# First block of a convolution and SiLU feed-forward kernel: the matrices' units from the third on issued from SP, the second block's input queued behind them

## The chip, the cores and the metric

One NeuronCore of one Trainium2 chip. The metric is device time in microseconds (us) of one execution; quoted times are medians of several runs. A profile is one execution taken by the hardware profiler; its span is 1.7 to 1.9 us shorter than the time of that run.

## The reference, cut to what matters

```python
# lightweight convolution along the sequence, 7 taps, one set of taps per head (8 heads of 24 channels)
out = np.einsum('hk,bskhg->bshg', softmax(weight), windows_of(x_padded))   # x: (8, 4096, 192)
# feed-forward on the 32768 rows of it
h = x @ w_in                          # w_in: (192, 2048), float64 as given
g = h * (1.0 / (1.0 + np.exp(-h)))    # SiLU
return (g @ w_out).astype(np.float32) # w_out: (2048, 192), float64 as given
```

The two weight matrices arrive as float64. The kernel loads their words and rounds them to float32 itself, in units: four for `w_in` and four for `w_out`.

## The kernel before

The 32768 rows are worked in 32 blocks of 1024. The first block is special. While TensorE multiplies it, the units of the matrices are still being loaded, rounded on VectorE and, for `w_in`, swapped between partition halves by a DMA (`ws<-wr`) that only the second block reads. From the second block on, everything is steady.

```python
tpool = tc.tile_pool(name="tp", bufs=3)   # raw words and rounding scratch share three buffers
psum  = tc.tile_pool(name="ps", bufs=8, space=PSUM)
...
def load(b):                 # input of block b: 12 loads of 64 KB in pieces of 128 bytes ("nat")
    ...
def load_in(j, queue):       # unit j of w_in: four loads of 192 KB ("raw")
    ...
def load_out(q, queue):      # unit q of w_out: two loads of 384 KB ("raw")
    ...
def round_in(j):
    rounded(wr[j]..., ("i", j), j < 2)              # VectorE (ScalarE helps for units 0 and 1)
    for e in range(2):
        nc.scalar.dma_start(                        # the swap, issued from ScalarE's queue
            out=ws[j][R * e : R * e + R], in_=wr[j][R - R * e : 2 * R - R * e])
...
def up_plain(b, j):          # matmuls of unit j into all 8 PSUM banks, then SiLU frees them
    ...
            if k == NK - 1:
                for e in range(2):
                    nc.scalar.activation(g[:, n, e, :], hs[a, n, e], AF.Silu)
...
load_in(0, nc.scalar)
load_in(1, nc.sync)
...
for k in range(NK):
    turn_in(0, k)            # transpose, convolve and spread ("dup") the first block's input
    ...
    spread(0, k)             # four SP copies of 128 KB
    if k == 0:
        round_in(0)
        load_in(2, nc.gpsimd)
round_in(1)
load_in(3, nc.gpsimd)
load(1)
for j in range(NJ):          # NJ = 4
    up_plain(0, j)
    if j + 2 < NJ:
        round_in(j + 2)
        load_out(j, nc.gpsimd)
    else:
        round_out(j + 2 - NJ)
        load_out(j, nc.gpsimd)
for j in range(2, NJ):
    round_out(j)
```

The text counts units from one: the "fourth unit" is `load_in(3)`, `round_in(3)`. In the profile, the lines are L123 (nat), L163 and L170 (raw), L109 (rounding), L217 (swap), L335 (dup), L373 (matmuls of `up_plain`), L383 (its SiLU), L503 (the first block's down projection), L409 and L464 (the steady blocks). A scheduler decides the order in each engine's queue.

Of the kernel before, what the change touches and what calls it, by code (L numbers as in the profile page):

```python
# [17 lines left out]
def kernel(  # L18
# [24 lines left out]
    nc = tc.nc  # L43
# [74 lines left out]
    def load(b):  # L118
        nat = nats[b] = xpool.tile([P, NK, TB // SQ, SQ], F32, tag="nat", name="nat")
        for k in range(NK):  # L120
            for i in range(P // SQ):
                c = R * k + SQ * (i % 2)
                (nc.sync if b or k or i % 2 else nc.scalar).dma_start(  # L123
                    out=nat[SQ * i : SQ * i + SQ, k, :, :],
                    in_=x_v[2 * b + i // 2][:, :, c : c + SQ],
                )
# [27 lines left out]
    def raw_tile(key):  # L154
        raws[key] = tpool.tile([P, 4 * TB], I32, tag="t", name="raw")[:, 0 : 2 * WC]
        return raws[key]

    def load_in(j, queue):
        raw = raw_tile(("i", j)).rearrange("p (a k c) -> p a k c", a=2, k=NK)
        for e in range(2):  # L160
            for a in range(2):
                c = 2 * P * (NM * a + 2 * j + e)
                queue.dma_start(  # L163
                    out=raw[R * e : R * e + R, a, :, :], in_=in32[:, :, c : c + 2 * P]
                )

    def load_out(q, queue):
        raw = raw_tile(("o", q)).rearrange("p (a e d) -> p a e d", a=2, e=2)
        for a in range(2):
            queue.dma_start(out=raw[:, a, :, :], in_=out32[a, q])  # L170
# [42 lines left out]
    def round_in(j):  # L213
        rounded(wr[j].rearrange("p a k c -> p (a k c)"), ("i", j), j < 2)

        for e in range(2):
            nc.scalar.dma_start(  # L217
                out=ws[j][R * e : R * e + R], in_=wr[j][R - R * e : 2 * R - R * e]
            )

    def round_out(q):
        rounded(wo[q].rearrange("p a e d -> p (a e d)"), ("o", q), False)
# [71 lines left out]
    def turn_in(b, k):  # L294
        if k == 0 and b:
            xt = xts[b] = xpool.tile([P, NK, pad + TB], F32, tag="xt", name="xt")
            if b * TT % S == 0:
                nc.gpsimd.memset(xt[0:R, :, 0:pad], 0.0)
            else:
                nc.gpsimd.tensor_copy(xt[0:R, :, 0:pad], tails.pop(b))  # L300
        xt = xts[b]
        pin(
            nc.vector.transpose(  # L303
                xt[:, k, pad : pad + TB], nats[b][:, k, :, :].rearrange("p k c -> p (k c)")
            )
        )
        if k == NK - 1:
            if b:
                nc.sync.dma_start(out=xt[R:P, :, 0:pad], in_=xt[0:R, :, TB : TB + pad])
            if (b + 1) * TT % S:  # L310
                tails[b + 1] = xpool.tile([R, NK, pad], F32, tag="tail", name="tail", bufs=2)
                nc.sync.dma_start(out=tails[b + 1], in_=xt[R:P, :, TB : TB + pad])

    def conv(b, k, i):

        src = xts[b][:, k, i : i + TB]
        dst = nats[b][:, k, :, :].rearrange("p k c -> p (k c)")
        tap = taps[:, k, i : i + 1]
        if i == 0:
            pin(nc.vector.tensor_scalar(dst, src, scalar1=tap, scalar2=None, op0=ALU.mult))  # L320
        else:
            pin(
                nc.vector.scalar_tensor_tensor(  # L323
                    out=dst, in0=src, scalar=tap, in1=dst, op0=ALU.mult, op1=ALU.add
                )
            )

    def spread(b, k):

        if k == 0:  # L330
            dups[b] = xpool.tile([P, 2, NK, TB], F32, tag="dup", name="dup")
        src = nats[b][:, k, :, :].rearrange("p k c -> p (k c)")
        for n in range(2):
            for e in range(2):
                nc.sync.dma_start(  # L335
                    out=dups[b][R * e : R * e + R, n, k, :], in_=src[R * n : R * n + R, :]
                )
# [25 lines left out]
    def up_plain(b, j):  # L363

        d = dups[b]
        outs = [(a, n) for a in range(2) for n in range(2)]
        hs = {(a, n, e): bank() for a, n in outs for e in range(2)}
        order = [(k, o) for k in range(NK) for o in outs]
        if j:
            order = [(k, o) for o in outs for k in range(NK)]  # L370
        for k, (a, n) in order:
            for e in range(2):
                nc.tensor.matmul(  # L373
                    hs[a, n, e],
                    rows(wr[j], e)[:, a, k, :],
                    rows(d, e)[:, n, k, :],
                    start=k == 0,
                    stop=k == NK - 1,
                )
            if k == NK - 1:  # L380
                for e in range(2):
                    g = g_tile(b, j, a)
                    nc.scalar.activation(g[:, n, e, :], hs[a, n, e], AF.Silu)  # L383
# [229 lines left out]
    for k in range(NK):  # L613
        turn_in(0, k)
        for i in range(K):
            conv(0, k, i)
        spread(0, k)
        if k == 0:
            round_in(0)
            load_in(2, nc.gpsimd)  # L620
    round_in(1)
    load_in(3, nc.gpsimd)
    load(1)
    for j in range(NJ):
        up_plain(0, j)
        if j + 2 < NJ:
            round_in(j + 2)
            load_out(j, nc.gpsimd)
        else:
            round_out(j + 2 - NJ)  # L630
            load_out(j, nc.gpsimd)
    for j in range(2, NJ):
        round_out(j)
    for s in plan[:NU]:
# [55 lines left out]
```

## Time and profile before

| | before |
|---|---|
| median of 3 runs | 2485.74 us (2484.02 to 2486.81) |
| span of the profiled run | 2482.4 us |
| TensorE busy | 2444.7 us (98%) |
| TensorE idle, all within the first 60 us | 21.5 + 1.84 + 0.31 + 2.51 + 1.35 us |
| half-clock stretches (before the last microseconds) | two, 29.96 to 33.37 and 43.62 to 47.03 us |

The lines on which the prediction rests stand in it. Four more lines of the timeline are needed later. Lines of the timeline give start and duration in us, then engine, line, operation and tile; in brackets stands the idle time before and what ended it. "ACTq" is an issue from ScalarE's queue.

```profile
39.84 1.12 ACTq L217 DMA_DIRECT2D ws<-wr  x2
40.99 1.28 ACT L383 ACT_TABLE_LOAD   x1 [5.01 <-DVE two L109]
42.28 4.03 ACT L383 ACTIVATE g<-ps 128x512 f32<-128x512 f32 x8
42.93 15.32 PE L373 MATMUL ps<-dup,wr 64*128 64x512 f32 x60 [2.51 <-ACT g L383]
```

The swap of the second unit sits in ScalarE's queue and waits for VectorE until 39.84. Only behind it come the table load and the first SiLU, and TensorE starts again at 42.93. The same pattern returns at 57.79 with the swap of the fourth unit; that is the wait the change is about.

### The profile page before, as it was taken

The numbers are of one execution on the slowest core, as the hardware profiler recorded it, in microseconds if no ns is written. First come the engines' busy times: TensorE is split into PE (matmuls) and PEld (weight loads), VectorE is DVE, ScalarE is ACT, GpSimd is POOL, SyncE is SP. The second block draws the span as 40 slices with busy tenths as digits, with TensorE's granted clock in tenths as the row PEclk, the third lists the DMA queues.
The fourth block names the chain that finished last, engine by engine and source line by source line (L and its number), as shares of the span: only waits on it lengthen the run. The fifth ranks groups of instructions, "written<-read, shape, count | busy, mean of one in ns | idle before, by whom it ended". The sixth has DMA issues, their size and how long they took to land.

```text
span 2482.4 us, 29776 instructions
## 1 busy us (share of the span) xinstructions
PE 2444.7 (98%) x11296; PEld 955.3 (38%) x11296; DVE 2043.7 (82%) x2748; ACT 968.8 (39%) x1747; POOL 69.9 (3%) x107
## 2 busy tenths in 40 slices
PE   5999999999999999999999999999999999999998
PEld 2334433344333344333433333443334433333332
DVE  8798888888888988888888889888888888898875
ACT  2144433344333444333443334443334433344432
POOL 3300000000000000000000000000000000000000
PEclk9999999999999999999999999999999999999999
DMA  7321122211222211222112222112221122221110
GB/s 149 73 47 31 35 52 51 41 37 35 43 52 43 46 32 35 51 52 40 38 35 43 52 43 47 31 35 52 51 40 38 34 43 52 43 45 33 35 39 13
DMA packets 450270, 110.78 MB, mean 45 GB/s; under 512 B 422304, under 2 KB 423968, under 8 KB 450128
## 3 DMA queue, kind: packets, MB, share of 16 engines
q1 hardware_dynamic: 444272, 101.26, 21.4%
q0 software_dynamic: 1600, 4.92, 0.8%
q10 hardware_dynamic: 4256, 2.72, 0.5%
q8 instruction: 88, 1.44, 0.3%
q14 instruction: 54, 0.44, 0.1%
HBM read 31.49 MB, written 25.17 MB: 23 GB/s over the span
## 4 chain that ended last, share of the span: by engine, by line
PE 97%; DVE 1%; DMA 1%; issue 0%; POOL 0%; ACTq 0%; ACT 0%; POOLq 0%; DVEq 0%
PE ps L409 47%; PE ps L464 47%; PE ps L503 2%; PE ps L373 1%; DVE two L109 0%; DVE nat L323 0%; DMA raw<-in_moe_w_in_dram 0%; DMA nat<-in_x_dram 0%; DVE mh L109 0%; DVE xt L303 0%; POOL raw L163 0%; DVE nat L320 0%; DVE u L550 0%; DVE cmb L550 0%; ACTq L217 0%
## 5 line engine op out<-in xcount | busy, mean ns | idle before, releaser
L464 PE MATMUL ps<-g,wo 128*64 128x512 f32 x2976 | 873.2, 593 | 0.0
L409 PE MATMUL ps<-dup,ws 64*128 64x512 f32 x2480 | 869.9, 589 | 0.0
L433 DVE TENSOR_TENSOR g<-u,ps 128x512 f32<-128x512 f32 x744 | 488.5, 680 | 117.0 <-PE ps L409 103.0
L409 PE MATMUL ps<-win,wr 64*128 64x512 f32 x1488 | 567.7, 589 | 0.0
L464 PEld LDWEIGHTS ps<-g,wo 128*64 128x64 f32 x2976 | 275.6, 137 | 572.2 <-issue 548.7
L430 ACT ACTIVATE g<-g 128x512 f32<-128x512 f32 x744 | 445.6, 631 | 88.1 <-DVE g L433 88.1
L409 PEld LDWEIGHTS ps<-dup,ws 64*128 64x128 f32 x2480 | 363.0, 187 | 292.0 <-issue 284.7
L464 PE MATMUL ps<-t,wx 128*64 128x512 f32 x992 | 466.1, 592 | 0.0
L323 DVE SCALAR_TENSOR_TENSOR nat<-xt,taps,nat 128x512 f32<-128x512 f32 x576 | 431.4, 749 | 11.9
L547 ACT COPY cmb<-ps 64x512 f32<-64x512 f32 (+1 forms) x93 | 54.1, 582 | 965.1 <-PE ps L464 964.3
L409 PE MATMUL ps<-dup,wr 64*128 64x512 f32 x992 | 419.9, 596 | 0.0
L424 ACT COPY u<-ps 128x512 f32<-128x512 f32 x496 | 278.2, 589 | 233.3 <-PE ps L409 233.0
L464 PE MATMUL ps<-t,wo 128*64 128x512 f32 x992 | 360.5, 592 | 0.0
L450 DVE TENSOR_TENSOR t<-g,t 128x1024 f32<-128x1024 f32 x248 | 303.6, 1224 | 60.6 <-PE ps L464 50.2
L409 PEld LDWEIGHTS ps<-win,wr 64*128 64x128 f32 x1488 | 233.4, 187 | 175.3 <-issue 146.9
L450 DVE TENSOR_TENSOR t<-g 128x1024 f32<-128x1024 f32 x248 | 299.3, 1218 | 0.0
L409 PE MATMUL ps<-win,ws 64*128 64x512 f32 x496 | 242.2, 589 | 0.0
L464 PE MATMUL ps<-g,wx 128*64 128x512 f32 x496 | 233.1, 592 | 0.0
L409 PEld LDWEIGHTS ps<-dup,wr 64*128 64x128 f32 x992 | 160.5, 187 | 127.4 <-issue 119.5
L424 DVE COPY u<-ps 128x512 f32<-128x512 f32 x248 | 166.3, 680 | 12.0 <-PE ps L409 8.3
L428 ACT ACTIVATE g<-ps 128x512 f32<-128x512 f32 x248 | 144.0, 596 | 79.3 <-PE ps L409 75.4
L559 DVE STREAM_TRANSPOSE osb<-cmb 128x512 f32<-128x512 f32 x96 | 67.5, 704 | 87.0 <-ACT cmb L547 79.0
(57 smaller groups left out, 1085.6 us busy)
## 6 DMA issues: line engine op xcount, KB each, us to landing
dup<-nat SPq DMA_DIRECT2D x384, 128.0 KB, 2.3
nat<-in_x_dram SPq DMA_DIRECT2D x382, 64.0 KB, 2.5
out_dram<-osb SPq DMA_DIRECT2D x378, 64.0 KB, 1.9
raw<-in_moe_w_out_dram POOLq DMA_DIRECT2D x8, 384.0 KB, 4.3
raw<-in_moe_w_in_dram POOLq DMA_DIRECT2D x8, 192.0 KB, 5.7
ws<-wr ACTq DMA_DIRECT2D x8, 192.0 KB, 5.1
raw<-in_moe_w_in_dram ACTq DMA_DIRECT2D x4, 192.0 KB, 5.5
raw<-in_moe_w_in_dram SPq DMA_DIRECT2D x4, 192.0 KB, 3.8
```

What stands on the lines that cost most here:

```text
L323: nc.vector.scalar_tensor_tensor(out=dst, in0=src, scalar=tap, in1=dst, op0=ALU.mult, op1=ALU.add)
L373: nc.tensor.matmul(hs[a, n, e], rows(wr[j], e)[:, a, k, :], rows(d, e)[:, n, k, :], start=k == 0, stop=k == NK - 1,)
L409: nc.tensor.matmul(bk[b, m, bn], rows(w, half), rows(v, half), start=first, stop=True, skip_group_check=True,)
L424: pin(copy(u, bk[b, m, "1"]))
L428: pin(nc.scalar.activation(g, bk[b, m, "1"], AF.Silu))
L430: pin(nc.scalar.activation(g, g, AF.Silu))
L433: pin(nc.vector.tensor_tensor(g, us.pop((b, m, i)), bk[b, m, bn], op=ALU.add))
L450: pin(nc.vector.tensor_tensor(t[i // 2][:, i % 2, :], u, v, op=ALU.subtract))
L464: nc.tensor.matmul(accs[b][i][R * half : R * half + R, :], lhs, rhs, start=first and j == 0, stop=j == NJ - 1, skip_group_check=True,)
L503: nc.tensor.matmul(acc[k][R * n : R * n + R, :], wo[j][:, a, e, R * k : R * k + R], gs[b, j, a][:, n, e, :], start=j == 0 and a == 0 and e ...
L547: pin(nc.scalar.copy(*copies[name]()))
L559: nc.vector.transpose(osb[:, i, :, :].rearrange("p k c -> p (k c)"), cmbs[b][0][:, i, :])
```

## The change

Its intent: issue the third and later units from SP and put the second block's input, which is needed only after 86 us, behind them in the same queue, so that its transfers no longer run beside those of the units. In the trace of before, the fourth unit's four loads landed 4.7 to 8.7 us after their issue, with nat issued from 37.73 to 51.89.

```diff
         if k == 0:
             round_in(0)
-            load_in(2, nc.gpsimd)
+            load_in(2, nc.sync)
     round_in(1)
-    load_in(3, nc.gpsimd)
-    load(1)
+    load_in(3, nc.sync)
     for j in range(NJ):
         up_plain(0, j)
         if j + 2 < NJ:
             round_in(j + 2)
-            load_out(j, nc.gpsimd)
+            load_out(j, nc.sync)
         else:
             round_out(j + 2 - NJ)
-            load_out(j, nc.gpsimd)
+            load_out(j, nc.sync)
+        if j == 1:
+            load(1)
```

## The prediction

Its sum is 0 + 0 - 1.6 + 0 = -1.6 us, so 2484.1 us. That nat's transfers hold back the raw words was the reading of two landing times, 8.7 and 3.8 us. That another issuer alone is worth nothing was an estimate from the issue times; e4 tests it.

> **What bounds the kernel now.** I read the page's busy shares first, then TensorE's waits, then the first 60 us in the timeline and the chain of work that ended last, and at the end the DMA view of the stretch that the change touches. The page says how much room there is at all:
>
> ```profile
> PE 2444.7 (98%) x11296; PEld 955.3 (38%) x11296; DVE 2043.7 (82%) x2748; ACT 968.8 (39%) x1747; POOL 69.9 (3%) x107
> PE   5999999999999999999999999999999999999998
> PE 97%; DVE 1%; DMA 1%; issue 0%; POOL 0%; ACTq 0%; ACT 0%; POOLq 0%; DVEq 0%
> ```
>
> TensorE works 2444.7 of 2482.4 us; only the first of forty slices (62 us) has a gap worth the name. The change touches only loads that are over by about 75 us. Even if it removed every TensorE wait of the start, it could not reach 2% (50 us). TensorE's own list of waits, over the whole span, has three kinds of idle in five places:
>
> ```profile
> PE ps L373 <- DVE wr L109: 21.5, 1, 21.5
> PE ps L373 <- ACT g L383: 3.9, 2, 2.5
> PE ps L373 <- DMA dup<-nat: 2.2, 2, 1.8
> ```
>
> The 21.5 us are the wait for the first matrix unit, which comes from the ACT queue and is not touched. The 2.2 us are the wait for the convolved input (gaps of 1.84 and 0.31). The 3.9 us are two waits for ScalarE's SiLU to free PSUM banks: 2.51 us at 42.93 and 1.35 us at 59.61. After 59.61 TensorE never waits again. So the question is which of these five waits the loads decide. The timeline (start, duration, engine, line, operation) answers for the last one:
>
> ```profile
> 39.11 2.63 POOL L163 DMA_DIRECT2D raw<-in_moe_w_in_dram  x4 [2.97 <-DVE two L109]
> 37.73 14.16 SPq L123 DMA_DIRECT2D nat<-in_x_dram  x12
> 50.05 1.07 DVE L109 TENSOR_SCALAR two<-raw 128x768 int32<-128x768 int32 x2 [3.27 <-DMA raw<-in_moe_w_in_dram]
> 56.80 0.96 DVE L109 SCALAR_TENSOR_TENSOR wr<-mh,two 128x768 f32<-128x768 f32 x1
> 57.79 1.12 ACTq L217 DMA_DIRECT2D ws<-wr  x2
> 58.96 5.00 ACT L383 ACTIVATE g<-ps 128x512 f32<-128x512 f32 x10 [9.90 <-DVE two L109]
> 59.61 10.62 PE L373 MATMUL ps<-dup,wr 64*128 64x512 f32 x47 [1.35 <-ACT g L383]
> ```
>
> Read it upwards. TensorE stands at 59.61 because SiLU had not freed banks. ScalarE could not, because its queue holds the swap of the fourth unit (ws<-wr) in front of the SiLUs, and that issue waits for VectorE to finish the unit at 57.76. VectorE began that unit only at 50.05, after 3.27 us idle for the raw words. Those were issued at 39.11 but landed at 49.83, as the chain that ended last says in one line:
>
> ```profile
> 41.12 8.70 DMA raw<-in_moe_w_in_dram
> ```
>
> Meanwhile SP issued the second block's input (nat, twelve loads, from 37.73), which nobody reads before 89.87.
>
> [...] this load took 8.7 us, while the raw loads of the second unit, issued on SP from 11.13 to 13.8 at the tail of the first nat, have a median of 3.8 us. [...] four issues take 2.57 to 2.63 us on POOL and 2.70 us on SP, so moving them alone is worth nothing; the order in the queue must do it. [...] the second unit's loads, issued at 20.71, had data moving by 22 us beside VectorE work. [...] the granted clock is 0.50 for about 3.4 us after the gaps of 1.84 and 2.51 us, and stays 1.00 after 1.35.
>
> ```profile
> 44.00:45.00 1.00, 1.00 (x4) 0.45 (x2) 1.00 (x2) 1.00 (x3) 0.00 (x0) 0.50 1.16 192
> 59.00:60.00 1.00, 0.39 (x1) 0.29 (x2) 1.00 (x3) 1.00 (x3) 1.00 (x2) 1.00 0.68 218
> ```
>
> (Columns: stretch, width, busy of PE, PEld, DVE, ACT, POOL, then granted clock, DMA share, GB/s.)
>
> **The change part by part.** The built order of the changed kernel shows no change in TensorE's, VectorE's or ScalarE's instructions. POOL loses its 16 issues; SP gains them, with nat split: two loads behind the fourth unit's raw words, three behind the first out-matrix unit, seven behind the second.
>
> Third unit's raw words: their buffer comes free at 20.4 us, and SP is idle from about 18.2 (its four copies issued) to 27.3. SP issues at about 20.5 instead of POOL at 20.71. Needed by VectorE at 39.84, landed long before in both: 0 us. Bytes in front of the next copies of the convolved input are 4x192 KB plus ws 2x192 KB, moved in both kernels; DMA was quiet by 27.4 and the copies issue at 27.3. So the 1.84 us gap should stay.
>
> Fourth unit's raw words: the buffer comes free at 39.1 as before (VectorE's read of the second unit), so four issues by 41.6. nat can no longer start at 37.73 and stands behind. In the way is only ws of the second unit (2x192 KB, issued 39.84 to 40.96). Estimate from this trace: 1152 KB (768 + 384) moved from 22.0 to 27.4 in the same mix with nothing else, 5.4 us; data starts about 1.2 us after the issue, as there; 39.1 + 1.2 + 5.4 = 45.7, plus at most 0.7 to 1.3 us for two nat loads of 64 KB at the 100 GB/s that nat shows alone at 39: 46 to 47. VectorE is ready at 46.78. So its idle of 3.27 us becomes 0 to 0.3.
>
> Then, all by about 3.2 us earlier: fourth unit finished at 54.5 instead of 57.76, ws issued by 55.7, SiLU from 55.8 instead of 58.96. TensorE needs the freed banks when? Its last matmul ended at 58.25 and lasts 0.59, so started at 57.66; pairs start every 0.43 (0.25 load and 0.18 pause in the PEld rows). The next was due at 58.09 and came at 59.61: lost 1.52 us. The next two pairs came at 0.48 instead of 0.43: 0.1. Of VectorE's 3.2 us only these 1.6 us reach TensorE; the rest becomes slack. There is margin: raw may land as late as 49.83 - 1.52 = 48.3 and TensorE still loses nothing.
>
> Gap at 42.93: ScalarE waits there for the second unit (VectorE done at 39.80), then loads its table (1.28 us). No changed load lies before it: unchanged, including the half clock after it (five pairs at about 0.8 us in place of 0.43: some 1.8 us that stay lost).
>
> Out-matrix units: needed by VectorE at about 54.5, 62.5, 71 and 79 in the new timing; their buffers come free at about 46, 53.6, 61 and 69, and they take 3.6 to 5.3 us to land. 0 us. nat: last seven behind the second of them, so issued by about 60 and landed by 67, needed at about 86.6: 0 us. GpSimd without its 2.6 us of issues can combine earlier; its results are read after 119: 0 us.
>
> Sum: 0 + 0 - 1.6 + 0 = -1.6 us. TensorE has no wait after 59.61, so the whole 1.6 us reach the end: 2485.74 - 1.6 = 2484.1 us.
>
> **Rivals.** (a) Nothing: nat was not the competitor; the eight loads of raw and ws need the time themselves. Then raw lands near 49 to 50 and the time stays 2485.7. Against it: the same mix took 5.4 us earlier; for it: ws of the third unit also ran from 46.81, too late to matter. (b) A new wait replaces the old: SP is one queue in order, and the issue for the fourth unit's words waits for VectorE at its head. [...] (c) nat too late: its tail waits for two VectorE steps. It would need 20 us of delay to reach TensorE. Hardly. (d) More than 1.6 us: [...] a half-clock stretch, worth about 1.8 us, in either direction and at two places (gaps at 27.7 and 40.4). This is not the change's doing, but it moves single runs: 2482.3 or 2486.
>
> **Range and chances.** The three runs before span 2484.02 to 2486.81, so the gain is smaller than the spread. Around 2484.1 I allow the loss of the gain and a half-clock stretch upwards, and one such stretch saved downwards: 2481.8 to 2486.6. Two per cent is 50 us; the whole start has less than 8 us of avoidable TensorE waits, so faster is 0.5%. Slower by 50 us would need a stall of a kind that no row shows: 0.5%. Within 2%: 99%.
>
> **What would show each step.** Right: VectorE's wait for the raw words (3.27 us) gone or below 0.5; the fourth unit's landing at 46 to 47 us; SiLU resuming near 55.8; TensorE's waits for SiLU down from 3.9 us in two to 2.5 in one; gaps of 21.5, 1.84, 0.31 unchanged; down projection (L503) starting near 76.7 instead of 78.31. Wrong: a longer wait for dup<-nat (rival b), the 1.35 us gap still there with raw landing past 48.3 (rival a), a wait of VectorE for nat after 86 us (rival c), or a different number of half-clock slices in the first 60 us (rival d).

## The result, and the profile after

| | before | after |
|---|---|---|
| median | 2485.16 us (4 runs, 2484.02 to 2486.81) | 2482.38 us (4 runs, 2480.33 to 2483.11) |
| ratio, 95% interval | | 0.9987 (0.9970 to 1.0004) |
| again | 2484.00 us (9 runs, 2483.74 to 2486.37) | 2481.78 us (5 runs, 2481.47 to 2482.92) |
| ratio, 95% interval | | 0.9989 (0.9975 to 1.0002) |

A ratio is the mean time of one kernel's fast runs over that of the other's fast runs of the same rounds, so it is not quite the ratio of the medians. Both intervals just include 1. But in each call every run of the changed kernel lies below every run of the kernel before, and the change is 2.2 to 2.8 us.

TensorE's waits over the whole span of the changed kernel, and VectorE's wait for the words of `w_in` (columns: who waited for what, us in total, times, longest):

```profile
PE ps L373 <- DVE wr L109: 21.3, 1, 21.3
PE ps L373 <- DMA dup<-nat: 3.9, 2, 2.4
PE ps L373 <- ACT g L383: 2.8, 1, 2.8
DVE two L109 <- DMA raw<-in_moe_w_in_dram: 0.6, 1, 0.6
```

VectorE's 3.27 us have become 0.6, and one of the two waits for SiLU is gone. But the wait for dup<-nat grew from 2.2 to 3.9. The timeline of the changed kernel answers to that of before:

```profile
29.38 4.82 PE L373 MATMUL ps<-dup,wr 64*128 64x512 f32 x16 [2.44 <-DMA dup<-nat]
35.63 4.62 PE L373 MATMUL ps<-dup,wr 64*128 64x512 f32 x16 [1.43 <-DMA dup<-nat]
38.83 2.71 SPq L163 DMA_DIRECT2D raw<-in_moe_w_in_dram  x4
41.64 1.46 SPq L123 DMA_DIRECT2D nat<-in_x_dram  x2
47.08 1.36 DVE L109 TENSOR_SCALAR two<-raw 128x768 int32<-128x768 int32 x2 [0.63 <-DMA raw<-in_moe_w_in_dram]
54.33 1.12 ACTq L217 DMA_DIRECT2D ws<-wr  x2
55.49 3.05 ACT L383 ACTIVATE g<-ps 128x512 f32<-128x512 f32 x6 [5.82 <-PE ps L373]
43.06 34.43 PE L373 MATMUL ps<-dup,wr 64*128 64x512 f32 x144 [2.80 <-ACT g L383]
```

The raw words are issued at 38.83 with nat behind them, their landings take 3.5 to 6.1 us instead of 4.7 to 8.7, and VectorE starts on them at 47.08 instead of 50.05. The swap of the fourth unit is issued at 54.33 instead of 57.79. From 43.06 on, all 144 matmuls of the remaining three units run in one piece; before, they were cut at 58.25.

The larger waits for dup are no later arrivals: the matmuls start at 29.38 and 35.63, against 29.51 and 35.78 before. TensorE only arrived sooner. Its first 16 matmuls took 5.67 us instead of 6.21 (TensorE starts matmuls in pairs; these start 0.85 us apart, twice the later 0.43, until about 25 us instead of 26; the clock column reads 1.00 there, but the traces' first clock records are at 25.27 us in the changed kernel and at 26.55 before), the next 16 took 4.82 instead of 5.95. For the latter the windows show why (busy time of TensorE in each stretch, then the granted clock, DMA share, GB/s; the first block of lines is before, the second the changed kernel):

```profile
29.00:34.00 5.00, 4.49 (x12) 0.66 0.36 81
43.00:50.00 7.00, 7.00 (x25) 0.76 1.06 196
56.00:66.00 10.00, 8.65 (x40) 1.00 0.45 119
```

```profile
29.00:34.00 5.00, 4.62 (x16) 1.00 0.35 78
43.00:50.00 7.00, 6.94 (x18) 0.56 1.02 240
56.00:66.00 10.00, 10.00 (x50) 1.00 0.82 192
```

This profiled run of the changed kernel had no half-clock stretch at 30 us, but a double one from 42.34 to 49.17: only 18 matmuls between 43 and 50 us, against 25. That is why its down projection starts just 0.89 us sooner (77.42 against 78.31), though 2.1 us of gap are gone: about 1.3 us more went to the half clock in this one run (by the matmul starts in the traces, pairs lost 3.1 us against 0.43 each after 43 us, and 1.9 before). After that nothing differs. From the second block's first matmul to the very last one there are 2351.91 us in both traces.

### The profile page after: what moved, and what is told of

Same layout as the page of the kernel before. It is cut to its first block, busy times and chain, and to the rows that moved or that the text cites. A ratio compares the mean times of both kernels' runs of the same rounds, so it can differ in the third digit from the quotient of the medians.

```text
span 2481.4 us, 29765 instructions
## 1 busy us (share of the span) xinstructions
PE 2443.3 (98%) x11296; PEld 964.3 (39%) x11296; DVE 2044.1 (82%) x2748; ACT 969.1 (39%) x1747; POOL 59.4 (2%) x91
## 4 chain that ended last, share of the span: by engine, by line
PE 98%; DVE 1%; DMA 0%; issue 0%; ACTq 0%; SPq 0%; ACT 0%; POOL 0%; POOLq 0%; DVEq 0%
PE ps L409 47%; PE ps L464 47%; PE ps L503 2%; PE ps L373 1%; DMA raw<-in_moe_w_in_dram 0%; DVE nat L323 0%; DVE two L109 0%; DVE mh L109 0%; SPq L123 0%; DVE xt L303 0%; DVE u L550 0%; DVE cmb L550 0%; ACT L383 0%; ACTq L217 0%; ACTq L123 0%
```

## The experiments

Ten runs were made, e1 and e10 of kernels seen already, each with five timed rounds against the kernel before; all gave correct results. The calls were e1 to e4, e5 to e8, and e9 with e10, each on another chip. Within each call the runs of before are shared: medians 2484.00, 2485.70 and 2485.70 us. Runs of different calls are best compared by their ratios. In all runs VectorE and TensorE have the same instructions in the same order, and ScalarE too but for the place of the swaps (by the order of the instructions in the traces).

| run | loads | swaps (units 2 to 4) | median us | ratio (95%) |
|---|---|---|---|---|
| e1 | as changed | ScalarE | 2481.78 | 0.9989 (0.9975 to 1.0002) |
| e2 | as before (same built order) | ScalarE | 2486.47 | 1.0005 (0.9992 to 1.0017) |
| e3 | fourth unit alone on SP | ScalarE | 2482.45 | 0.9991 (0.9979 to 1.0004) |
| e4 | units on POOL, nat behind them on POOL | ScalarE | 2481.68 | 0.9990 (0.9978 to 1.0003) |
| e5 | as before | units 3, 4 on POOL | 2481.04 | 0.9984 (0.9972 to 0.9997) |
| e6 | on SP, nat ahead of the fourth unit | ScalarE, fourth behind 8 SiLUs | 2481.60 | 0.9986 (0.9973 to 0.9998) |
| e7 | as changed | POOL | 2476.66 | 0.9965 (0.9951 to 0.9978) |
| e8 | as changed | SP | 2476.66 | 0.9965 (0.9953 to 0.9978) |
| e9 | as before | POOL | 2478.54 | 0.9973 (0.9960 to 0.9987) |
| e10 | as changed (same as e7) | POOL | 2476.68 | 0.9967 (0.9955 to 0.9980) |

The theory: nat's loads delay the fourth unit's raw words (4.7 to 8.7 us from issue to landing before, 3.5 to 6.1 in the changed kernel); the words delay VectorE; VectorE delays the swap; and the swap, at the head of ScalarE's queue, holds back the SiLUs that free TensorE's banks. Rivals: the difference is only where the half-clock stretches fell (e1, e2); SP as the issuer is what helps (e4); other parts of the change bring it (e3); TensorE waits on the words by another way than the swap (e5, e6).

**e1, the changed kernel again.** No edit.

> The changed kernel once more, unaltered, with more rounds, because its gain is about as large as the spread of the runs. Theory (the fourth unit's raw words reach SBUF before VectorE needs them, so ScalarE's queue no longer stands behind the swap and TensorE's gap before the third unit's matmuls is gone): 1.5 to 3 us faster than before, ratio 0.9988 to 0.9994. In the profile one TensorE wait for SiLU instead of two. Rival (the difference seen so far is only where half-clock stretches fell): ratio 0.9997 to 1.0003.

Measured: 2.2 us in the medians, all five runs under all nine of before, one wait of TensorE for SiLU (2.7 us). The gain is real. By its interval alone it would not be proven.

**e2, the load of nat merely written later.**

```diff
     load_in(3, nc.gpsimd)
-    load(1)
     for j in range(NJ):
         ...
+        if j == 1:
+            load(1)
```

> The second block's input written later in the program, as in the change, but all units stay on the POOL queue. The built order of every engine is the same as before, since nothing stands ahead of that input in SP's queue. So this is the kernel before against itself: ratio 1.000 within 0.0006, VectorE's wait for the raw words 3 to 3.5 us, TensorE's second wait for SiLU 1.2 to 1.5 us. A theory in which writing the load later is by itself enough expects the gain of the change here.

Measured: ratio 1.0005, VectorE's wait 2.8 us (a little under what was expected), TensorE's second wait 3.0 us, twice what was expected. The built order is the same as before, and that is the first finding: with nothing in front of it in SP's queue, the load written later keeps its place. The second finding is in the profile of this run, which is the kernel before with its half-clock stretches elsewhere (timeline, then windows):

```profile
42.91 13.63 PE L373 MATMUL ps<-dup,wr 64*128 64x512 f32 x60 [2.64 <-ACT g L383]
59.56 20.98 PE L373 MATMUL ps<-dup,wr 64*128 64x512 f32 x81 [3.02 <-ACT g L383]
```

```profile
29.00:34.00 5.00, 4.65 (x16) 1.00 0.34 76
43.00:50.00 7.00, 7.00 (x33) 1.00 1.05 193
56.00:66.00 10.00, 6.98 (x18) 0.66 0.49 119
```

Here TensorE had full clock from 43 to 50 us (1.00) and finished its 60 matmuls 1.7 us sooner. It gained nothing by it: the next start is 59.56, against 59.61 before, because VectorE and the swap set that moment. It waited 3.02 us instead, and after that longer gap came about 6.8 us of half clock (an estimate from the 0.66 over the 10 us from 56 to 66). So in these two profiles of the kernel before, a slow stretch at 43 us is swallowed by the gap, and a quick one is paid back after it. The span of this profile is 2485.2 us, against 2482.4 of the other. Runs of before lie near 2484 or near 2486; that the place of the half-clock stretches makes the difference is the author's guess, and only two profiles bear on it.

**e3, the fourth unit alone on SP.**

```diff
-    load_in(3, nc.gpsimd)
+    load_in(3, nc.sync)
     load(1)
```

> The kernel before with one part of the change alone: only the fourth in-matrix unit is issued from SP, so that the second block's input stands behind it in that queue; third unit and out-matrix units stay on POOL, and the input's twelve loads follow without interruption. Theory (the one queue position is the whole effect): raw words landed at 46.5 to 47.5 us, VectorE waits under 1 us, no second SiLU wait of TensorE, as fast as the changed kernel within 0.5 us (ratio to before 0.9988 to 0.9994). Rival (the other moves, third unit or out-matrix units off POOL, bring part of it): less than half of the gain, ratio 0.9996 or more.

Measured: VectorE's wait 0.8 us, one wait for SiLU (2.5 us), median 2482.45, 1.6 us under before and 0.7 above e1; the ratios (0.9991 and 0.9989) do not tell these two apart. This one line brings most of the gain, perhaps all. Its half-clock stretches lie where before's do (granted clock 0.66 from 29 to 34 us and 0.76 from 43 to 50 in both), and the down projection starts 2.26 us sooner (76.05 against 78.31). Of this, 0.16 us were there before the gap (restart at 42.77 against 42.93); the other 2.10 are the gap's cost with the half clock alike.

**e4, units left on POOL, nat behind them on POOL.**

```diff
-    load(1)
     for j in range(NJ):
         ...
+        if j == 1:
+            load(1, nc.gpsimd)
```

> All units stay on POOL as before, and the second block's input is issued from POOL too, behind the fourth unit. So the order is that of the changed kernel, without its queue. Theory (order decides, not which queue issues): raw words landed by 47.5, VectorE waits under 1 us, TensorE's second SiLU wait gone, gain 1.5 to 2.5 us. Rival [...]: VectorE still waits over 2 us and the SiLU wait stays. The combines on POOL run later here (its queue holds seven input loads until the second out-matrix unit has space), which nothing before 119 us reads, so no loss from it.

Measured: VectorE's wait 0.4 us; TensorE's second SiLU wait 0.17 us; median 2481.68. No unit from the third on was issued from SP, and the gain is the same (2481.78 in e1): nat is issued from POOL at 41.59, behind the unit, as it was from SP at 41.64 in the changed kernel. So here the queue's order decides, not which engine issues. (VectorE waited 3.2 us later for an out-matrix unit; that did not reach TensorE.)

**e5, before with the swaps of units three and four issued from POOL.**

```diff
-            nc.scalar.dma_start(
+            (nc.gpsimd if j > 1 else nc.scalar).dma_start(
                 out=ws[j][R * e : R * e + R], in_=wr[j][R - R * e : 2 * R - R * e]
             )
```

> The kernel before, all loads as before, but the swaps (ws<-wr) of the third and fourth unit are issued from POOL instead of ScalarE's queue. Theory (the late raw words reach TensorE only through the swap that stands ahead of the SiLUs in ScalarE's queue): VectorE still waits about 3 us for the raw words, yet TensorE's second SiLU wait is gone and the time is that of the changed kernel, 1.5 to 3 us under before. Rival (TensorE waited for the fourth unit itself or for VectorE in some other way): the gap near 59 us stays, ratio 0.9997 or more.

From the waits and the timeline of this run:

```profile
DVE two L109 <- DMA raw<-in_moe_w_in_dram: 2.7, 1, 2.7
43.19 31.65 PE L373 MATMUL ps<-dup,wr 64*128 64x512 f32 x144 [2.68 <-ACT g L383]
```

VectorE still waits 2.7 us for the late words, yet TensorE runs its 144 matmuls in one piece. The median is 2481.04 us, with the loads of before; its ratio to before, 0.9984, is like that of the changed kernel (0.9987 and 0.9989) or a little better. The swap's place in ScalarE's queue is the link.

**e6, nat put ahead of the fourth unit on SP.**

```diff
-            load_in(2, nc.gpsimd)
+            load_in(2, nc.sync)
     round_in(1)
-    load_in(3, nc.gpsimd)
     load(1)
+    load_in(3, nc.sync)
     ...              # load_out(j, nc.gpsimd) becomes load_out(j, nc.sync), both
```

> Units three and four and the out-matrix units on SP as in the change, but the second block's input written ahead of the fourth unit: in SP's queue one of its four loads, then the twelve input loads, then its other three. In this build the swap of the fourth unit also stands behind eight SiLUs of the second unit in ScalarE's queue instead of two. Theory of the queue order: the raw words land later than in any other kernel, after 50 us, and VectorE waits 4 us or more. Theory of the swap's place: TensorE all the same has no second SiLU wait and gains 1.5 to 2.5 us. If instead late words alone cost TensorE, it is slower than before by 1 us or more.

Waits and timeline of this run:

```profile
DVE two L109 <- DMA raw<-in_moe_w_in_dram: 9.7, 1, 9.7
50.36 3.03 SPq L163 DMA_DIRECT2D raw<-in_moe_w_in_dram  x3
63.17 1.12 ACTq L217 DMA_DIRECT2D ws<-wr  x2
64.98 11.05 PE L373 MATMUL ps<-dup,wr 64*128 64x512 f32 x48 [0.54 <-ACT g L383]
```

The last three loads wait for nat until 50.36, the last of them lands at 56.4, and VectorE stands for 9.7 us, three times as long as before. Yet the kernel is as fast as the changed one (2481.60; ratio 0.9986). The scheduler put the fourth swap behind eight SiLUs of the second unit, so the banks were freed in time; only 0.54 us of wait is left (1.3 us by the matmul starts), where TensorE meets the swap's delay at the start of its fourth unit. So in this run the words' lateness, 9.7 us, reaches TensorE through the swap alone, with 0.54 us of wait; an early arrival was never needed in itself.

**e7 and e8, the changed kernel with the swaps of units two to four issued from POOL, or from SP.**

```diff
-            nc.scalar.dma_start(
+            (nc.gpsimd if j else nc.scalar).dma_start(      # e8: nc.sync
```

> The changed kernel with the swaps of units two to four issued from POOL, so ScalarE's queue holds no issue between the rounding of the second unit and the SiLUs. Theory: ScalarE loads its table at about 36.5 us instead of 41 and starts SiLU by 38; the wait of 2.5 to 2.8 us near 43 us falls under 1 us, with fewer half-clock stretches after it: another 2.5 to 5 us, 2477 to 2479.5 us, ratio to before 0.9970 to 0.9980. Rival (the first SiLU wait comes from the table load or from the second unit's rounding itself): no gain over the changed kernel.

> As the run before, but these swaps are issued from SP. The second unit's swap then stands behind the first of the four loads of the fourth unit and the other three stand behind the swap, which waits for VectorE until 39.8 us; the fourth unit's words so land about 1 us later and VectorE waits up to 2 us. Theory: TensorE gains as in the run before (ratio 0.9970 to 0.9980), since nothing of it stands in ScalarE's queue. Rival (one queue for all delays unit four enough to reach TensorE): 1 us or more slower than the run with the swaps on POOL.

Timeline of e7:

```profile
36.22 1.28 ACT L383 ACT_TABLE_LOAD   x1
37.51 4.03 ACT L383 ACTIVATE g<-ps 128x512 f32<-128x512 f32 x8
35.88 35.26 PE L373 MATMUL ps<-dup,wr 64*128 64x512 f32 x160 [0.23 <-DMA dup<-nat]
```

The table is loaded at 36.22 instead of 40.99, SiLU starts at 37.51, and TensorE runs without a wait from 35.88 to the end. Both versions take 2476.66 us, 9.0 us under before and a little below the expected range for e7; they beat both kernels. Sharing SP with the units cost nothing in e8, where VectorE did not wait for the words at all; up to 2 us had been expected.

**e9 and e10, the fourth corner: loads of before with the moved swaps, beside e7 again.** e9 is the kernel before with the edit of e7.

> The kernel before, loads untouched (third and fourth unit and out-matrix units on POOL, the second block's input on SP ahead of them in time), with the swaps of units two to four moved from ScalarE's queue to POOL's. It fills the fourth corner: loads old or new, swaps old or new. Theory (the loads' order acts only through the swap in ScalarE's queue): with the swaps gone from there the load change is worth nothing, so this runs as fast as the changed kernel with moved swaps, 2476 to 2477.5 us, ratio to before 0.9960 to 0.9972, though VectorE still waits 3 us or more for the raw words. Rival (the two changes add up): 2478.5 to 2480 us.

> The changed kernel with the swaps of units two to four on POOL once more, beside the run before on the same chip, to compare the two directly: 2476.5 to 2477 us. Theory: within 0.5 us of the run before. Rival (the loads still matter): 1.5 us or more faster than it.

Measured: 2478.54 against 2476.68 us. The expectation that the load change is worth nothing once the swaps are gone is wrong: 1.9 us of it stay, and both rivals came true as they were written (e9 at 2478.5 to 2480; e10 faster by 1.5 us or more). The traces show a new place for part of it. In e9 VectorE is about 3.2 us behind from 50 us to the end of the first block, and TensorE is now early enough to meet that lateness in the second. Timeline of e9, then of e7 (SP's copy of the convolution's border, xt<-xt, and the VectorE instruction that needs it):

```profile
126.92 0.63 SPq L309 DMA_DIRECT2D xt<-xt  x1
128.91 0.49 DVE L320 TENSOR_SCALAR nat<-xt,taps 128x512 f32<-128x512 f32 x1 [1.66 <-DMA xt<-xt]
```

```profile
123.66 0.63 SPq L309 DMA_DIRECT2D xt<-xt  x1
126.85 0.48 DVE L320 TENSOR_SCALAR nat<-xt,taps 128x512 f32<-128x512 f32 x1
```

SP comes to that copy 3.3 us later in e9, VectorE stands for 1.66 us, and near 131.4 us TensorE's matmul starts fall behind by 0.4 us; in e7, and in every other profile that was laid beside it, that stretch has no such loss (2351.91 us from second block to last matmul, in e9 2352.34). The end of the program, from the last matmul's start, takes 10.6 to 10.7 us in profiles without units on POOL (after, e1, e6, e7, e8, e10) and 10.85 to 11.37 in those with them (before, e2 to e5, e9), some 0.15 to 0.8 us more for no reason that the trace gives. Together that is about 1 us; the other 0.9 us between the medians of e9 and e10 stay open. (The profiled runs of e9 and e7 are 1.62 us apart, and there nothing stays open: 0.32 stand at the second block's first matmul, 0.26 of it already at the very first matmul, so not from these loads; 0.43 come in that block, 0.65 at the end, and 0.22 lie outside the spans.)

## Why the prediction was right or wrong

The measured median of 2482.38 lies in the range, 1.7 us under the 2484.1 predicted; the class (within 2%) is as forecast.

- **What bounds it; no way to 2%:** right. Only the first 60 us moved.
- **Fourth unit's words at 46 to 47 us, VectorE's idle down to 0 to 0.3:** right in the landing (the last words landed at 46.95, VectorE started at 47.08), slightly off in the idle: 0.63 us, and 0.4 in e1, just outside or inside the stated sign of "below 0.5". e4, with 0.4, confirms that the order, not the issuing engine, does it. One reading of the lines is misnamed: the loads issued at 20.71 are the third unit's, not the second's.
- **SiLU from 55.8:** 55.49.
- **TensorE's gap worth 1.6 us:** the right mechanism, a term mis-sized. The step took the due time from the last matmul's start (57.66) plus one pair's 0.43. But that matmul was the first of a pair. Its partner was due at 57.67, which is 0.43 after the second of the pair before (57.24), and not at 58.09. The gap cost 1.94 + 0.16 = 2.1 us by the matmul starts in the trace of before, not 1.52 + 0.1. The idle time of a wait understates its cost here because the idle time begins at the last matmul's end, 0.59 us after its start, while its partner was due with that start: a wait of 1.35 us cost 2.1 us, and by the same count 0.54 us cost 1.3 (e6) and 0.17 us cost 0.9 (e4). e3, with its half-clock stretches in the same places, shows the same 2.10 us between the restart near 43 us and the down projection.
- **Down projection near 76.7:** 77.42 in the changed kernel, with a half-clock stretch of 6.83 us instead of 3.41 after 42 us; 76.05 in e3.
- **All of it reaches the end:** right; 2351.91 us follow in both. The end of the program is 0.15 us shorter besides (10.85 to 10.70), which was not foreseen.
- **Gaps 1.84 and 0.31 unchanged:** wrong as numbers (2.44 and 1.43), right in what was meant: the starts at 29.38 and 35.63 did not move by more than 0.15 us, and e2 shows the same larger gaps (2.58 and 1.46) with the loads of before.
- **Rival (d), the half-clock stretches:** present, and misjudged in one respect. They were treated as noise that adds to either kernel alike. In the kernel before, VectorE fixed the restart (59.61 with a half clock at 43 us, 59.56 in e2 without one), so that half clock was absorbed by the gap; without the gap it counted in full (from the restart near 43 us to the down projection, e3 with one such stretch takes 33.28 us and e5 with none 31.58). That is why the profiled pair shows a gain of only 1.0 us in its spans.
- **Deadline of 48.3 us for the words:** right only for the given order in ScalarE's queue. e6 missed it by 8 us and lost less than before did (1.3 us by the matmul starts, against 2.1), at a later place, since its swap stands six SiLUs further back. The deadline also holds only with the half clock where that trace has it: in e4, whose 60 matmuls from 42.80 took 13.63 us (the same as in e2 at a granted clock of 1.00; 15.32 before), TensorE came to this point about 1.8 us sooner and waited 0.17 us (0.9 by the matmul starts), though the words had landed at 47.14.
- **The 2.51 us wait stays:** right for this change (2.80). e7 shows that it had the same cause, a swap in ScalarE's queue.

## What to carry to other kernels

When a compute engine also issues DMAs, look at what each such issue waits for: here ScalarE's other instructions stood behind the blocked issue too, for 5.01 us, and taking the issues to another queue was worth more than making their data come sooner (alone 7.2 us in e9, against 2.2 to 2.8 for the loads, each against before in its own call). Here the load that nobody needed yet was held back by what stood before it in its queue (nat issued at 41.64 in the changed kernel and 41.59 in e4, against 37.73 before), not by being written later (e2, with the built order of before); check the built order. And where a gap ends at a moment that another engine sets, time gained or lost before it may not count (1.7 us gained in e2, and the restart at 59.56 against 59.61), so read a gap's cost from start to due start between profiles with the half clock in the same places, and time small gains over many runs.

## What the traces leave open

- The half clock. The stretches in the first 60 us are 3.41 us long in the kernel before and 6.83 us in the changed kernel. In the profile of before they came after TensorE's gaps of 1.84 and 2.51 us and not after 1.35; in that of the changed kernel none came after 2.44 and 1.43, and the one of 6.83 began at 42.34, still inside the gap of 2.80. So the length of a gap does not sort these cases; what decides is not shown.
- The longer program end with units issued from POOL (10.85 to 11.37 us from the last matmul's start, against 10.6 to 10.7 without); its cause is not shown.
